# Decode attention, forward and backward: V transposes moved behind the K scores, fp32-pair transposes, and O and dq by wide matmuls

## The chip, the cores and the metric

The kernel runs on one core of one Trainium2 chip. The metric is the device time of one execution in microseconds. A profiled execution also has a span, from its first to its last instruction, which is a little shorter than its time.

## The reference

One query row meets 8192 keys in each of 32 heads, in bfloat16. The kernel returns the attention output O and the gradients of q, k and v.

```python
B, H, Sq, Skv, Dh = 1, 32, 1, 8192, 128
scores = jnp.einsum('bhqd,bhkd->bhqk', q, k) * q.shape[-1] ** -0.5
attn = softmax(scores)                        # p
out  = jnp.einsum('bhqk,bhkd->bhqd', attn, v) # O
out, vjp = jax.vjp(f, q, k, v); grads = vjp(grad_out)
```

Written out for one head, with dO for `grad_out`: dp = V dO, ds = p (dp - dO.O) x scale, dq is the sum of ds times the rows of K, dK is the outer product of ds and q, and dV the outer product of p and dO. A head reads K and V, 2.1 MB each, and writes dK and dV, 2.1 MB each; all else is small.

## The kernel before, in words

A head's K (or V) lies in SBUF as a tile of 128 partitions x 64 slots x 128 features: partition `p` holds the rows 64p to 64p+63. Softmax weights and scores of a head are 128 x 64. The loop (lines 228 to 296) runs over the heads, one more time than there are heads: iteration h works on head h up to dp, and finishes head h-1 (ds, dq, dK). The order of all instructions is the order of the source, since a manual schedule is entered at line 125; each engine takes its own instructions in that order.

In one iteration:

- VectorE transposes K in blocks of 32 x 32 words (`k_blocks`, line 133), and TensorE makes the K scores of it by 64 matmuls of four moving columns (`k_scores`, line 145). A mask on VectorE (`s_mask`, line 151) and eight short matmul passes (`s_swap`, line 161) put the scores in place.
- V has to be transposed on TensorE for dp, since V is contracted over features there. `v_transposes` (lines 165 to 172) does a quarter of the head: 16 transposes of 128 x 128 bfloat16 into a PSUM tile `T_ps` (two buffers), and one copy by ScalarE into `XT_sb` (three buffers). `v_scores` (line 180) then makes 16 columns of dp, by one matmul each, with dO as a moving operand of one column. Before the change the first two quarters of V's transposes stand ahead of the K scores, the other two after the softmax.
- The maximum over partitions goes by a diagonal matrix and an fp32 matmul with ones (`diag`, lines 251 to 254, and `nbias`, line 265). ScalarE makes the exponentials `e` and their row sums `rs` (line 268); an fp32 matmul with ones gives the whole sum (line 271), VectorE its reciprocal `rinv`, ScalarE the weights `p_rep`, each repeated R = 4 times (line 280).
- O of a head and dq of the head before come from `contract` (line 185): 64 matmuls each, V or K as the stationary operand of 128 x 128, one moving column. dq stands in two halves between the softmax steps; O stands between the third and fourth V transposes. A matmul with a broadcast dO (line 288) gives dO.O to all partitions.
- VectorE makes dK and dV in quarters (`outer`, line 195). After the second and the fourth quarter the SyncE queue stores half of the tensor (1.05 MB, line 203).

All DMAs are issued by SyncE, in source order. In the steady state its order in one iteration is: dK store, K load for head h+2 (line 258), dK store, dV store, V load for head h+2 (line 294), dV store. A load waits until its buffer is free: three buffers hold K, two hold V. A DMA further back on SyncE's queue waits behind it. K and V of the first two heads are asked for ahead of the loop, head 0 in four parts, and so is V of the last head.

Of the kernel before, what the change touches and what calls it, by code (L numbers as in the profile page):

```python
# [11 lines left out]
BF16 = mybir.dt.bfloat16  # L12
F32 = mybir.dt.float32
PSUM = bass.MemoryType.PSUM

CH = 16
R = 4
# [7 lines left out]
def kernel(  # L25
# [11 lines left out]
    nc = tc.nc  # L37
    P = 128
    _, H, S, D = k.shape
    assert D == P and S % (P * CH) == 0 and H <= P  # L40
    NT = S // P
# [3 lines left out]
    W = D // 2  # L45
# [3 lines left out]
    consts = ctx.enter_context(tc.tile_pool(name="consts", bufs=1))  # L49
# [3 lines left out]
    tpool = ctx.enter_context(tc.tile_pool(name="tsb", bufs=3))  # L53
    gpool = ctx.enter_context(tc.tile_pool(name="gen", bufs=2))
    small = ctx.enter_context(tc.tile_pool(name="small", bufs=2))
    psT = ctx.enter_context(tc.tile_pool(name="psT", bufs=2, space=PSUM))
# [4 lines left out]
    Kt, Vt, XK, XV, st = {}, {}, {}, {}, {}  # L61
# [9 lines left out]
    def load_k(h):  # L71
        Kt[h] = kpool.tile([P, NT, D], BF16, tag="K", name="Kt")
        parts = NCH if h == 0 else 1
        for c in range(parts):
            nc.sync.dma_start(slots(Kt[h], c, parts), rows_of(k, h, c, parts))  # L75

    def load_v(h):
        Vt[h] = vpool.tile([P, NT, D], BF16, tag="V", name="Vt")
        parts = NCH if h in (0, H - 1) else 1
        for c in range(parts):  # L80
            nc.sync.dma_start(slots(Vt[h], c, parts), rows_of(v, h, c, parts))

    rows = consts.tile([H, 2, D], BF16)
# [7 lines left out]
    ident = consts.tile([P, P], BF16)  # L91
    make_identity(nc, ident[:])
    ident_f = consts.tile([P, P], F32)
# [10 lines left out]
    for w in range(NB):  # L104
        for e2 in range(2):
            four = consts.tile([H, NQ, QD], BF16, tag=f"four{w}{e2}")
# [3 lines left out]
            tp = psT.tile([P, CH, P], BF16, tag="T")  # L110
# [1 line left out]
            nc.vector.tensor_tensor(  # L112
                q_blk[:, :, 2 * w + e2, :], tp[:, 0, 0:H].unsqueeze(2).to_broadcast([P, H, NQ]),
                in_quad[:].unsqueeze(1).to_broadcast([P, H, NQ]), op=ALU.mult)
    doT = consts.tile([P, H], BF16)
    do_f = consts.tile([P, H], F32)
    tp = psT.tile([P, CH, P], BF16, tag="T")
    nc.tensor.transpose(tp[:, 0, 0:H], rows[:, 1, :], ident[0:H, 0:H])
    nc.vector.tensor_copy(doT[:], tp[:, 0, 0:H])
    nc.vector.tensor_copy(do_f[:], doT[:])  # L120

    o_all = consts.tile([P, H], F32)
    dq_all = consts.tile([P, H], F32)
# [39 lines left out]
                             start=True, stop=True, skip_group_check=True)  # L163

    def v_transposes(h, c):
        T_ps = psT.tile([P, CH, P], BF16, tag="T", name="T_ps")
        for i in range(CH):
            nc.tensor.transpose(T_ps[:, i, :], Vt[h][:, c * CH + i, :], ident[:])  # L168
        X = tpool.tile([P, CH, P], BF16, tag="XT", name="XT_sb")
        nc.scalar.copy(X.rearrange("p c s -> p (c s)").bitcast(F32),  # L170
                       T_ps.rearrange("p c s -> p (c s)").bitcast(F32))
        XV[h, c] = X

    def v_scores(h, c):
        X = XV.pop((h, c))
        if c == 0:
            st[h]["dp"] = psD.tile([P, 512], F32, tag="dp", name="dp_ps")
        for i in range(CH):
            n = c * CH + i
            nc.tensor.matmul(st[h]["dp"][:, n:n + 1], lhsT=X[:, i, :], rhs=doT[:, h:h + 1],  # L180
                             start=True, stop=True, skip_group_check=True)

    def contract(Xt, rep, out_col, first=0, last=NT):
        for n in range(first, last):
            nc.tensor.matmul(out_col, lhsT=Xt[:, n, :], rhs=rep[:, n, 0:1],  # L185
                             start=(n == 0), stop=(n == NT - 1), skip_group_check=True)

    def outer(h, which, r):
        x = st[h]
        if r == 0:  # L190
            x[which] = gpool.tile([P, NT, D], BF16, tag=which, name="G_" + which)
        G, dst = x[which], out_2 if which == "dk" else out_3
        rep, row = x["ds"] if which == "dk" else x["p"], x["qd"][:, 0 if which == "dk" else 1, :]
        Q = NT // 4
        nc.vector.tensor_tensor(  # L195
            slots(G, r, 4).rearrange("p n (a b) -> p n a b", b=R),
            slots(rep, r, 4).unsqueeze(2).to_broadcast([P, Q, D // R, R]),
            row.rearrange("p (a b) -> p a b", b=R).unsqueeze(1).to_broadcast([P, Q, D // R, R]),
            op=ALU.mult)
        parts = 4 if h == H - 1 else NST  # L200
        if r % (4 // parts) == 4 // parts - 1:
            c = r // (4 // parts)
            nc.sync.dma_start(rows_of(dst, h, c, parts), slots(G, c, parts))

    def rows_bc(h):
        x = st[h]
        nc.tensor.matmul(x["m"][:, 256:512], lhsT=ident[0:H, h:h + 1].to_broadcast([H, P]),  # L207
                         rhs=rows[:].rearrange("h a d -> h (a d)"), start=True, stop=True,
                         skip_group_check=True)
        x["qd"] = small.tile([P, 2, D], BF16, tag="qd", name="qd")  # L210
        nc.scalar.copy(x["qd"][:].rearrange("p a d -> p (a d)"), x["m"][:, 256:512])
# [7 lines left out]
            out=x["ds"][:], in0=x["dp"][:, 0:NT].unsqueeze(2).to_broadcast([P, NT, R]), scalar=pdt[:],  # L219
            in1=x["p_s"][:].unsqueeze(2).to_broadcast([P, NT, R]), op0=ALU.subtract, op1=ALU.mult)  # L220

    def dq_of(h, half):
        out = st[h]["dp"][:, 128:129]
        contract(Kt[h], st[h]["ds"], out, half * NT // 2, (half + 1) * NT // 2)
        if half == 1:
            nc.scalar.copy(dq_all[:, h:h + 1], out)  # L226

    for h in range(H + 1):
        p_ = h - 1
        if h < H:  # L230
            x = st[h] = {}
            for u in range(NCH):
                k_blocks(h, u)
            v_transposes(h, 0)
            v_transposes(h, 1)
            k_scores(h)
            v_scores(h, 0)
        if h > 0:
            ds_of(p_)
            outer(p_, "dk", 0)  # L240
        if h < H:
            s_mask(h)
            s_swap(h)
        if h > 0:
            dq_of(p_, 0)
            outer(p_, "dk", 1)
        if h < H:
            mx = small.tile([P, 1], F32, tag="mx")
            nc.vector.reduce_max(mx[:], x["sn"], axis=AX.X)  # L249
            diag = small.tile([P, P], F32, tag="diag")  # L250
            nc.vector.tensor_scalar(diag[:], ident_f[:], mx[:], scale, op0=ALU.mult, op1=ALU.mult)  # L251
            x["m"] = psM.tile([P, 512], F32, tag="m", name="m_ps")
            nc.tensor.matmul(x["m"][:, 128:256], lhsT=ones_f[:], rhs=diag[:], start=True, stop=True,  # L253
                             skip_group_check=True)
        if h > 0:
            dq_of(p_, 1)
        if 0 < h and h + 2 < H:
            load_k(h + 2)
        if h > 0:
            outer(p_, "dk", 2)  # L260
        if h == 0:
            load_k(2)
        if h < H:
            nbias = small.tile([P, 1], F32, tag="nbias")
            nc.vector.tensor_reduce(nbias[:], x["m"][:, 128:256], axis=AX.X, op=ALU.max, negate=True)
            e = small.tile([P, NT], F32, tag="e")
            rs = small.tile([P, 1], F32, tag="rs")
            nc.scalar.activation(e[:], x["sn"], ACT.Exp, bias=nbias[:], scale=scale, accum_out=rs[:])
            rows_bc(h)
            v_scores(h, 1)  # L270
            nc.tensor.matmul(x["m"][:, 0:1], lhsT=ones_f[:], rhs=rs[:], start=True, stop=True,  # L271
                             skip_group_check=True)
        if h > 0:
            outer(p_, "dk", 3)
        if h == H:
            break
        rinv = small.tile([P, 1], F32, tag="rinv")
        nc.vector.reciprocal(rinv[:], x["m"][:, 0:1])  # L278
        x["p"] = small.tile([P, NT, R], BF16, tag="prep", name="p_rep")
        nc.scalar.activation(x["p"][:], e[:].unsqueeze(2).to_broadcast([P, NT, R]), ACT.Copy, scale=rinv[:])  # L280
        x["p_s"] = small.tile([P, NT], F32, tag="p_s", name="p_s")
        nc.vector.tensor_scalar(x["p_s"][:], e[:], rinv[:], scale, op0=ALU.mult, op1=ALU.mult)
        v_transposes(h, 2)
        contract(Vt[h], x["p"], x["m"][:, 2:3])
        nc.scalar.copy(o_all[:, h:h + 1], x["m"][:, 2:3])
        v_scores(h, 2)
        v_transposes(h, 3)
        nc.tensor.matmul(x["m"][:, 1:2], lhsT=do_f[:, h:h + 1].to_broadcast([P, P]), rhs=o_all[:, h:h + 1],
                         start=True, stop=True, skip_group_check=True)
        v_scores(h, 3)  # L290
        outer(h, "dv", 0)
        outer(h, "dv", 1)
        if h + 2 < H:
            load_v(h + 2)
        outer(h, "dv", 2)
        outer(h, "dv", 3)

# [2 lines left out]
    for src, dst in ((o_all, out_0), (dq_all, out_1)):  # L300
        half = small.tile([P, H], BF16, tag="half")
# [36 lines left out]
```

## Time and profile before

| | |
|---|---|
| median of 12 runs | 675.89 us (673.4 to 679.41) |
| the profiled execution: time | 676.35 us |
| its span | 674.6 us |
| mean granted TensorE clock | 0.574 |
| bytes read from and written to HBM | 134.23 MB and 134.23 MB, 398 GB/s over the span |
| busy: PE, weight loads (PEld), DVE, ACT | 522.3, 495.7, 508.7, 175.8 us |
| V transposes (line 168) | 2048, 232.2 us busy, 310 ns each from start to end |
| ScalarE's copies of them (line 170) | 128, 1012 ns each |
| dK and dV multiplies (line 195) | 256, about 1220 ns each |
| K block transposes (line 133) | 128, 1213 ns each |
| one-column matmuls for O and dq (line 185) | 2 x 2048, 165 ns each from start to end |

PE, DVE, ACT and SP are TensorE, VectorE, ScalarE and SyncE. A group's line in the profile gives the source line, the engine, the operation, the tile written and the tiles read. Since matmuls overlap, the time from start to end of one is longer than the distance between two; the busy time of PE is the union of them, and it is not a measure of how much of the array's throughput is used. The granted clock is the share of full speed that TensorE was given. A wait names the engine and line that waited, what ended the wait, the total in us, how many times, and the longest. The DMA share is the mean busy share of the core's 16 DMA engines. The chain is followed backwards from the last instruction, at each step to what released it.

### The profile page before, as it was taken

To read this page: it belongs to the slowest core of one execution; us is meant where nothing else is said; L and a number is where in the kernel's file an instruction comes from. 1 tells how busy PE (TensorE), PEld (TensorE's weight loads), DVE (VectorE), ACT (ScalarE), POOL (GpSimd) and SP (SyncE) were. 2 spreads that over 40 slices of the span, in tenths; PEclk is the share of its full clock that TensorE was granted. 3 is DMA by queue.
4 is the path that set the end of the run, shared out by engine and by line. 5 is a ranking of instruction groups with operands and counts; after the bars stand their busy time and mean duration, and the time that the engine had idled before them with its cause. 6 is when DMAs were issued, how large, how long until landed. Compare 5 with 4: busy or idle time off the path is not lost.

```text
span 674.6 us, 23039 instructions
## 1 busy us (share of the span) xinstructions
PE 522.3 (77%) x10727; PEld 495.7 (73%) x10727; DVE 508.7 (75%) x658; ACT 175.8 (26%) x321; POOL 0.7 (0%) x6
## 2 busy tenths in 40 slices
PE   3899898877779777779767787778877778666991
PEld 3888887867778777778667786767867678666881
DVE  4789888777787777877777866787677886669683
ACT  1333223222323222222222222223222222222330
POOL 0000000000000000000000000000000000000000
PEclk9555556666556665566655565556666555655565
DMA  8999999999999999999999999999999999999874
GB/s 335 420 417 421 425 426 422 427 425 425 425 427 423 426 426 424 426 424 418 423 409 394 387 413 393 397 389 397 416 405 408 410 394 409 395 392 380 341 319 179
DMA packets 29808, 269.96 MB, mean 400 GB/s; under 512 B 3472, under 2 KB 3472, under 8 KB 6032
## 3 DMA queue, kind: packets, MB, share of 16 engines
q1 hardware_dynamic: 29712, 268.48, 97.2%
q8 instruction: 84, 1.38, 0.8%
q14 instruction: 12, 0.10, 0.0%
HBM read 134.23 MB, written 134.23 MB: 398 GB/s over the span
## 4 chain that ended last, share of the span: by engine, by line
DMA 51%; PE 39%; DVE 6%; issue 1%; ACT 1%; SPq 0%
DMA Vt<-in_v_dram 51%; PE T_ps L168 20%; PE m_ps L185 5%; PE s_ps L145 5%; DVE G_dk L195 4%; PE dp_ps L180 3%; PE dp_ps L185 2%; PE m_ps L253 2%; PE m_ps L271 2%; DVE sm L151 1%; PE m_ps L207 1%; ACT XT_sb L170 1%; DVE diag L251 1%; DVE mx L249 0%; SPq L75 0%
## 5 line engine op out<-in xcount | busy, mean ns | idle before, releaser
L168 PE MATMUL T_ps<-ident,Vt 128*128 128x128 bf16 x2048 | 232.2, 310 | 86.3 <-DMA Vt<-in_v_dram 85.7
L168 PEld LDWEIGHTS <-Vt 128*128 128x128 bf16 x2048 | 215.3, 149 | 89.1 <-DMA Vt<-in_v_dram 88.3
L170 ACT COPY XT_sb<-T_ps 128x1024 f32<-128x1024 f32 x128 | 129.6, 1012 | 293.7 <-PE T_ps L168 293.7
L195 DVE TENSOR_TENSOR G_dk<-ds_rep,qd 128x2048 bf16<-128x2048 bf16 x128 | 155.7, 1219 | 1.1
L195 DVE TENSOR_TENSOR G_dv<-p_rep,qd 128x2048 bf16<-128x2048 bf16 x128 | 148.2, 1221 | 9.1 <-ACT p_rep L280 8.8
L133 DVE STREAM_TRANSPOSE XK_sb<-Kt 128x1024 f32<-128x1024 f32 x128 | 148.1, 1213 | 2.8 <-DMA Kt<-in_k_dram 2.8
L151 DVE TENSOR_TENSOR sm<-s_ps,in_quad 128x256 f32<-128x256 f32 x32 | 13.6, 425 | 107.4 <-PE s_ps L145 107.4
L180 PE MATMUL dp_ps<-doT,XT_sb 128*128 128x1 bf16 x2048 | 73.8, 165 | 26.8 <-ACT XT_sb L170 24.9
L180 PEld LDWEIGHTS <-XT_sb 128*128 128x128 bf16 x2048 | 64.1, 103 | 37.5 <-ACT XT_sb L170 27.6
L185 PEld LDWEIGHTS <-Kt 128*128 128x128 bf16 x2048 | 63.6, 102 | 6.9 <-issue 2.5
L185 PE MATMUL dp_ps<-ds_rep,Kt 128*128 128x1 bf16 x2048 | 64.6, 165 | 1.4 <-issue 0.9
L185 PEld LDWEIGHTS <-Vt 128*128 128x128 bf16 x2048 | 61.1, 105 | 0.0
L185 PE MATMUL m_ps<-p_rep,Vt 128*128 128x1 bf16 x2048 | 60.5, 166 | 0.0
L145 PE MATMUL s_ps<-q_blk,XK_sb 128*128 128x4 bf16 x2048 | 57.7, 167 | 0.0
L145 PEld LDWEIGHTS <-XK_sb 128*128 128x128 bf16 x2048 | 57.6, 100 | 0.0
L226 ACT COPY dq_all<-dp_ps 128x1 f32<-128x1 f32 x32 | 5.1, 159 | 136.1 <-PE dp_ps L185 136.1
L253 PE MATMUL m_ps<-diag,ones_f 128*128 128x128 f32 x64 | 24.3, 482 | 11.1 <-DVE diag L251 11.1
L253 PEld LDWEIGHTS m_ps<-diag,ones_f 128*128 128x128 f32 x64 | 15.2, 296 | 13.9 <-DVE diag L251 13.9
L280 ACT ACTIVATE p_rep<-e,rinv 128x256 bf16<-128x256 f32 x32 | 16.2, 508 | 29.9 <-DVE rinv L278 29.9
L278 DVE RECIPROCAL rinv<-m_ps 128x1 f32<-128x1 f32 x32 | 5.4, 169 | 24.1 <-PE m_ps L271 24.1
L218 DVE SCALAR_TENSOR_TENSOR ds_rep<-dp_ps,pdt,p_s 128x256 bf16<-128x256 f32 x32 | 15.5, 484 | 4.4 <-PE dp_ps L180 1.1
L271 PE MATMUL m_ps<-rs,ones_f 128*128 128x1 f32 x64 | 18.5, 358 | 0.3 <-issue 0.3
(40 smaller groups left out, 161.8 us busy)
## 6 DMA issues: line engine op xcount, KB each, us to landing
Kt<-in_k_dram SPq DMA_DIRECT2D x31, 2048.0 KB, 22.1
out_dram<-G_dv SPq DMA_DIRECT2D x62, 1024.0 KB, 23.5
out_dram<-G_dk SPq DMA_DIRECT2D x62, 1024.0 KB, 20.0
Vt<-in_v_dram SPq DMA_DIRECT2D x30, 2048.0 KB, 25.3
Vt<-in_v_dram SPq DMA_DIRECT2D x8, 512.0 KB, 13.8
Kt<-in_k_dram SPq DMA_DIRECT2D x4, 512.0 KB, 5.3
out_dram<-G_dv SPq DMA_DIRECT2D x4, 512.0 KB, 11.6
out_dram<-G_dk SPq DMA_DIRECT2D x4, 512.0 KB, 9.6
```

Source lines behind the costliest of these rows:

```text
L133: nc.vector.transpose(XK[h][:, :, :, u, :], slots(Kt[h], u, NCH).rearrange("p g d -> p (g d)").bitcast(F32).rearrange("p (g w j) -> p g w ...
L145: nc.tensor.matmul(out[:, g, :], lhsT=cols[:, g, c // 2, c % 2], rhs=q_blk[:, h, c, :], start=(c == 0), stop=(c == 2 * NB - 1), skip_group ...
L151: nc.vector.tensor_tensor(x["sm"][:], x["s"][:, 0:NT].rearrange("p (a g) -> p a g", a=NQ).unsqueeze(2) .to_broadcast([P, NQ, NCH, CH]), in ...
L168: nc.tensor.transpose(T_ps[:, i, :], Vt[h][:, c * CH + i, :], ident[:])
L170: nc.scalar.copy(X.rearrange("p c s -> p (c s)").bitcast(F32), T_ps.rearrange("p c s -> p (c s)").bitcast(F32))
L180: nc.tensor.matmul(st[h]["dp"][:, n:n + 1], lhsT=X[:, i, :], rhs=doT[:, h:h + 1], start=True, stop=True, skip_group_check=True)
L185: nc.tensor.matmul(out_col, lhsT=Xt[:, n, :], rhs=rep[:, n, 0:1], start=(n == 0), stop=(n == NT - 1), skip_group_check=True)
L195: nc.vector.tensor_tensor(slots(G, r, 4).rearrange("p n (a b) -> p n a b", b=R), slots(rep, r, 4).unsqueeze(2).to_broadcast([P, Q, D // R, ...
L218: nc.vector.scalar_tensor_tensor(out=x["ds"][:], in0=x["dp"][:, 0:NT].unsqueeze(2).to_broadcast([P, NT, R]), scalar=pdt[:], in1=x["p_s"][: ...
L253: nc.tensor.matmul(x["m"][:, 128:256], lhsT=ones_f[:], rhs=diag[:], start=True, stop=True, skip_group_check=True)
L271: nc.tensor.matmul(x["m"][:, 0:1], lhsT=ones_f[:], rhs=rs[:], start=True, stop=True, skip_group_check=True)
L280: nc.scalar.activation(x["p"][:], e[:].unsqueeze(2).to_broadcast([P, NT, R]), ACT.Copy, scale=rinv[:])
```

## The change

The K scores come first in an iteration, and all V transposes come after the softmax weights. dq is dealt out in four unequal parts (4, 5, 4 and 3 of 16 matmuls) between the softmax steps. V is transposed as 32-bit words that hold two neighbouring features: 32 transposes of 128 x 128 words take the place of 64, and `v_scores` reads the even and the odd halves of the words, with `do_blk`, a zero-padded dO, so that two matmuls add up to two columns of dp. The number of those matmuls (64) stays.

O and dq go by `contract_wide`: four columns of weights (one for each of four slots) are stationary, and four slots of V or K (512 columns) move, 16 matmuls a head, into four rows of a whole PSUM bank: the bank of the head's scores for O, that of dp for dq. The four diagonal blocks of 128 are wanted; `gather_wide` copies the four rows to SBUF by ScalarE and adds the blocks by four fp32 matmuls. The last head keeps the old `contract`. V of head h+1 is loaded at the start of iteration h, behind both dV stores of head h-1, in place of V of head h+2 between the dV stores of head h. The K load stands after the fourth part of dq.

```diff
     def v_transposes(h, c):
-        T_ps = psT.tile([P, CH, P], BF16, tag="T", name="T_ps")
-        for i in range(CH):
-            nc.tensor.transpose(T_ps[:, i, :], Vt[h][:, c * CH + i, :], ident[:])
-        X = tpool.tile([P, CH, P], BF16, tag="XT", name="XT_sb")
-        nc.scalar.copy(X.rearrange("p c s -> p (c s)").bitcast(F32),
-                       T_ps.rearrange("p c s -> p (c s)").bitcast(F32))
+        T_ps = psT.tile([P, CH // 2, P], F32, tag="T", name="T_ps")
+        words = Vt[h].rearrange("p n d -> p (n d)").bitcast(F32)
+        for i in range(CH // 2):
+            m = c * CH // 2 + i
+            nc.tensor.transpose(T_ps[:, i, :], words[:, m * P:(m + 1) * P], ident_f[:])
+        X = tpool.tile([P, CH // 2, P], F32, tag="XT", name="XT_sb")
+        nc.scalar.copy(X[:], T_ps[:])
...
+    def contract_wide(Xt, rep, bank, first, last):
+        for g in range(first, last):
+            nc.tensor.matmul(bank[0:R, :], lhsT=rep[:, R * g:R * (g + 1), 0],
+                             rhs=Xt[:, R * g:R * (g + 1), :].rearrange("p n d -> p (n d)"),
+                             start=(g == 0), stop=(g == NT // R - 1), skip_group_check=True)
+
+    def gather_wide(bank, out_col):
+        four = small.tile([R, R, D], F32, tag="four", name="four")
+        nc.scalar.copy(four[:].rearrange("a b d -> a (b d)"), bank[0:R, :])
+        for b in range(R):
+            nc.tensor.matmul(out_col, lhsT=four[:, b, :], rhs=ident_f[0:R, b:b + 1],
+                             start=(b == 0), stop=(b == R - 1), skip_group_check=True)
...
+    def dq_of(h, part):
+        dp, cuts = st[h]["dp"], (0, 4, 9, 13, 16)
+        if h < H - 1:
+            contract_wide(Kt[h], st[h]["ds"], dp, cuts[part], cuts[part + 1])
+            if part == 3:
+                gather_wide(dp, dp[:, 128:129])
+        else:
+            contract(Kt[h], st[h]["ds"], dp[:, 128:129], 4 * cuts[part], 4 * cuts[part + 1])
+        if part == 3:
+            nc.scalar.copy(dq_all[:, h:h + 1], dp[:, 128:129])
...
-            v_transposes(h, 0)
-            v_transposes(h, 1)
             k_scores(h)
-            v_scores(h, 0)
+            if 0 < h < H - 1:
+                load_v(h + 1)
...
+        broad = h < H - 1
+        v_transposes(h, 0)
+        if broad:
+            contract_wide(Vt[h], x["p"], x["s"], 0, 4)
+        else:
+            contract(Vt[h], x["p"], x["m"][:, 2:3])
+        v_transposes(h, 1)
+        if broad:
+            contract_wide(Vt[h], x["p"], x["s"], 4, 8)
+        v_scores(h, 0)
         v_transposes(h, 2)
-        contract(Vt[h], x["p"], x["m"][:, 2:3])
+        if broad:
+            contract_wide(Vt[h], x["p"], x["s"], 8, 12)
+        v_scores(h, 1)
+        v_transposes(h, 3)
+        if broad:
+            contract_wide(Vt[h], x["p"], x["s"], 12, 16)
+            gather_wide(x["s"], x["m"][:, 2:3])
         nc.scalar.copy(o_all[:, h:h + 1], x["m"][:, 2:3])
         v_scores(h, 2)
-        v_transposes(h, 3)
```

On TensorE an iteration is then: K scores, dq part 0, the swap of scores, dq part 1, the maximum's matmul, the rows of q and dO (`rows_bc`), dq part 2, the sum's matmul, dq part 3, the gather of dq, and then V transposes and O by quarters with dp between them, the gather of O, dO.O, and the rest of dp.

More of the change, by code (lines that the diff above doesn't have):

```diff
@@ L114 @@
                 in_quad[:].unsqueeze(1).to_broadcast([P, H, NQ]), op=ALU.mult)
-    doT = consts.tile([P, H], BF16)
+    do_blk = consts.tile([P, H, 2, 2], BF16)
+    nc.vector.memset(do_blk[:], 0.0)
+    for e2 in range(2):
+        twice = consts.tile([H, 2, W], BF16, tag=f"twice{e2}")
+        nc.vector.tensor_copy(
+            twice[:], rows[:, 1, :].rearrange("h (j e) -> h e j", e=2)[:, e2:e2 + 1, :].to_broadcast([H, 2, W]))
+        tp = psT.tile([P, CH, P], BF16, tag="T")
+        nc.tensor.transpose(tp[:, 0, 0:H], twice[:].rearrange("h t j -> h (t j)"), ident[0:H, 0:H])
+        for t in range(2):
+            nc.vector.tensor_copy(do_blk[t * W:(t + 1) * W, :, e2, t], tp[t * W:(t + 1) * W, 0, 0:H])
     do_f = consts.tile([P, H], F32)
@@ L118 @@
     nc.tensor.transpose(tp[:, 0, 0:H], rows[:, 1, :], ident[0:H, 0:H])
-    nc.vector.tensor_copy(doT[:], tp[:, 0, 0:H])
-    nc.vector.tensor_copy(do_f[:], doT[:])
+    nc.vector.tensor_copy(do_f[:], tp[:, 0, 0:H])
     o_all = consts.tile([P, H], F32)
@@ L165, in v_transposes @@
     def v_transposes(h, c):
-        T_ps = psT.tile([P, CH, P], BF16, tag="T", name="T_ps")
-        for i in range(CH):
-            nc.tensor.transpose(T_ps[:, i, :], Vt[h][:, c * CH + i, :], ident[:])
-        X = tpool.tile([P, CH, P], BF16, tag="XT", name="XT_sb")
-        nc.scalar.copy(X.rearrange("p c s -> p (c s)").bitcast(F32),
-                       T_ps.rearrange("p c s -> p (c s)").bitcast(F32))
+        T_ps = psT.tile([P, CH // 2, P], F32, tag="T", name="T_ps")
[5 more added lines that the diff above has]
+        nc.scalar.copy(X[:], T_ps[:])
         XV[h, c] = X
     def v_scores(h, c):
-        X = XV.pop((h, c))
+        X = XV.pop((h, c)).rearrange("p m s -> p (m s)").bitcast(BF16).rearrange("p (m s e) -> p m e s", s=P, e=2)
         if c == 0:
             st[h]["dp"] = psD.tile([P, 512], F32, tag="dp", name="dp_ps")
[L178 to L181, printed above, removed]
+        for i in range(CH // 2):
+            n = c * CH + 2 * i
+            for e2 in range(2):
+                nc.tensor.matmul(st[h]["dp"][:, n:n + 2], lhsT=X[:, i, e2, :], rhs=do_blk[:, h, e2, :],
+                                 start=(e2 == 0), stop=(e2 == 1), skip_group_check=True)
     def contract(Xt, rep, out_col, first=0, last=NT):
@@ L220, in ds_of @@
             in1=x["p_s"][:].unsqueeze(2).to_broadcast([P, NT, R]), op0=ALU.subtract, op1=ALU.mult)
[L222 to L226, printed above, removed]
+    def dq_of(h, part):
[8 more added lines that the diff above has]
+            nc.scalar.copy(dq_all[:, h:h + 1], dp[:, 128:129])
     for h in range(H + 1):
@@ L240 @@
             outer(p_, "dk", 0)
+            dq_of(p_, 0)
         if h < H:
@@ L244 @@
         if h > 0:
-            dq_of(p_, 0)
+            dq_of(p_, 1)
             outer(p_, "dk", 1)
@@ L254 @@
                              skip_group_check=True)
+            rows_bc(h)
         if h > 0:
[L256 to L259, printed above, removed]
+            dq_of(p_, 2)
             outer(p_, "dk", 2)
@@ L268 @@
             nc.scalar.activation(e[:], x["sn"], ACT.Exp, bias=nbias[:], scale=scale, accum_out=rs[:])
-            rows_bc(h)
-            v_scores(h, 1)
             nc.tensor.matmul(x["m"][:, 0:1], lhsT=ones_f[:], rhs=rs[:], start=True, stop=True,
@@ L273 @@
         if h > 0:
+            dq_of(p_, 3)
+            if h + 2 < H:
+                load_k(h + 2)
             outer(p_, "dk", 3)
@@ L292 @@
         outer(h, "dv", 1)
-        if h + 2 < H:
-            load_v(h + 2)
         outer(h, "dv", 2)
```

## The prediction

> **What bounds the kernel now.** I read the page first: the slices, the DMA queues and the chain.
>
> ```profile
> DMA  8999999999999999999999999999999999999874
> q1 hardware_dynamic: 29712, 268.48, 97.2%
> DMA 51%; PE 39%; DVE 6%; issue 1%; ACT 1%; SPq 0%
> ```
>
> The 16 DMA engines are full from the second slice to the 37th, and the chain runs through loads of V more than through any engine. Next I cut the span at starts of V transposes that had waited for V (every fourth head), and asked for engines, clock and DMA in each stretch.
>
> ```profile
> 201.63:283.92 82.29, 65.05 (x1340) 61.80 (x1341) 63.32 (x81) 21.79 (x40) 0.00 (x0) 0.58 1.01 425
> 367.61:453.29 85.68, 66.12 (x1340) 62.72 (x1341) 63.20 (x81) 21.77 (x40) 0.00 (x0) 0.52 1.00 396
> ```
>
> Columns: length, busy PE, weight loads, DVE, ACT, POOL, then clock, DMA share, GB/s. Four heads take 82.3 us (20.6 each) at 425 GB/s and 85.7 (21.4) at 396; the DMA share is 1.0 in both, so the head's 8.39 MB set the period. DVE has 15.8 us of work in a head. How far behind TensorE is, the waits tell:
>
> ```profile
> PE T_ps L168 <- DMA Vt<-in_v_dram: 85.7, 27, 4.5
> DVE sm L151 <- PE s_ps L145: 107.4, 32, 5.1
> ```
>
> 27 heads begin with about 3.2 us of waiting for V. In the first heads, not yet waiting, the chain has V transposes start at 27.20, 44.77 and 62.18: TensorE's own head is 17.4 us. So TensorE has 3 to 4 us to spare in a head, DVE 5, and the DMA none. The last V transposes that wait for their load start at 623.47; from there to the end (674.6) it is 51.1 us of engine work and a last store.
>
> [...]here six such windows of one head, of which I show four:
>
> ```profile
> 242.62:246.04 3.42, 3.27 (x31) 3.28 (x32) 1.85 (x4) 1.01 (x1) 0.00 (x0) 0.50 1.00 426
> 246.04:249.45 3.41, 3.29 (x123) 3.11 (x121) 1.56 (x3) 1.01 (x1) 0.00 (x0) 1.00 1.04 440
> 249.45:252.86 3.41, 3.03 (x59) 2.58 (x57) 2.88 (x5) 0.73 (x4) 0.00 (x0) 0.50 0.99 416
> 252.86:256.27 3.41, 3.41 (x82) 3.41 (x83) 2.93 (x5) 1.52 (x2) 0.00 (x0) 0.50 1.03 435
> ```
>
> 31 transposes (128 moving columns each) in a window bring clock 1.00 in the next; 123 matmuls of 1 to 4 columns bring 0.50 after it, though PE is "busy" in both. [...]A window from 454.25 with 25 transposes was followed by 1.00, one from 556.65 with 21 was not. [...]16 transposes in 1.73 us are 108 ns each.[...]
>
> **The change, part by part, in one head of TensorE.** Removed: 64 V transposes, 64 x 108 ns = 6.9 us; 2 x 64 one-column matmuls for O and dq, 2 x 1.68 us (chain rows of L185 x64) = 3.4 us. Together 10.3 us of the 17.4.
>
> Added: (a) 32 fp32 transposes. Rows for fp32 (L253, L271) show two passes for a matmul and some 214 ns from one pass to the next, whether 1 or 128 columns move[...]. Lower end 107 ns at half clock (one pass, load hidden), next 213 (load bound), upper 427 (two passes); I take 160, at full clock 80: 5.1 or 2.6 us. (b) 2 x 16 wide matmuls: 32 x 427 = 13.7 us at half clock, 32 x 216 = 6.9 at full. (c) Two gathers: each stops TensorE for ScalarE's copy of 4 x 512 words (between the 1012 ns of 1024 and the 159 ns of 1: 0.6 us, and 0.3 + 0.2 for the signals), then 4 fp32 matmuls of two passes: 8 x 214 = 1.7 us, estimate 0.9 at full clock. So 2.0 to 2.8 us each. All V transposes and O of the head are queued behind the first, the do.O matmul behind the second. On ScalarE p_rep is queued behind the dq copy, hence VectorE's dV multiplies too; VectorE's 5 us cover that. (d) dp stays 64 matmuls of 25 ns, now two columns wide: nothing.
>
> Sums, the two stages of a head as they stand in the new order. K stage at full clock: scores 1.65, mask and swap 0.9, maximum and diagonal 0.8, its matmul 0.6, bias, exp and sum 1.9, dq's last part 0.65, gather 2.0, some 0.5 of signals: 9.0 us; dq's other 13 matmuls (2.8 us) lie under VectorE's answers. V stage at full clock: transposes 2.6, O 3.5, dp 1.7, gather 2.0, do.O 0.5, wait for p_rep 0.3: 10.6. Sum 19.6 us; with transposes at 107 ns even at full clock, 20.4. At half clock only: K stage 13, V stage 16.5, 29.5 us.
>
> The clock decides. Wide matmuls and transposes fill the windows of the V stage, so the full clock comes there, but a window late: up to 3.4 us at half clock, 1.7 us lost. Whether the K stage (16 x 216 = 3.5 us of moving columns in 9.0) keeps it no row says[...]. I take the loss of one window in two heads of three: 19.6 + 1.15 = 20.75 us.
>
> **What moves besides.** V's load for head h+1 is asked for at the start of head h, behind both dV stores of h-1 instead of between them; on SP's queue it passes one store of 1.05 MB, 2.6 us later. But it is needed only in the V stage, some 32 us after its buffer is free instead of 20: the 85.7 us of waiting for V go. What is late next is TensorE itself. K's load still stands between the dK stores; it waits for dq's last part, 7 to 9 us into a head, as now (251.61 against 242.76). ScalarE's copies of transposes keep size and number; two copies of 0.6 us a head fit in its 74% idle time. The extra do_blk set-up (some 7 short VectorE copies of 0.17 to 0.2 us) costs 1.2 us at most, once, and lies partly beside K's first load. Bytes are the same.
>
> **Sum.** Start of scores 13 us (now transposes at 10.84, scores 14.0); head 0 without dq 20.75 - 2 = 18.75; 30 heads x 20.75 = 622.5; last head, O by the old narrow way, 19; last dq and dK 6 and last store 10, as now (658.9 to 674.6). Span 689.3. The profiled execution has a span of 674.6 and a time of 676.35, 1.75 outside; so 691 us. Its time lies 0.46 above the median of the 12 runs (675.89), which I neglect.
>
> **Rivals.**
> - A, the forecast: TensorE is the bound, at 20 to 21.5 us a head. For it: added work (at best 2.6 + 6.9 + 4.0 against 10.3 removed) uses up the 3 us that V's wait shows to be free. Own range 676 to 712. Chance 0.42.
> - B, the other side: the DMA stays the bound and the end shortens. From V's last awaited landing it is V stage 10.6, K stage 9, V stage 9, 6 and 10 = 44.6 us instead of 51.1; less 2.6 for the store that V now follows: 674.6 - 3.9 + 1.75 = 672 us. It decides if TensorE's head stays below the DMA's 19.7 to 21.4 us: full clock throughout, and transposes under 80 ns. Against it: the first half, at 425 GB/s, leaves nothing above 19.7. At the start V(2) is asked for 5 us later, under 5 us of stores; bare, that would cost up to 5 and end it level. The fall from 425 to 396 GB/s with the DMA share unchanged might also give way to another order of transfers, or grow; I count nothing. Range 664 to 678, chance 0.33.
> - C: the K stage falls back to half clock in every head, its streams then taking 11 to 12 us, and the V stage starts cold: 12. At 23.5 us a head 13 + 21.5 + 705 + 21 + 16 = 776.5, so 778; heads between A and C give 715 to 780. Chance 0.22.
> - D: fp32 transposes in two passes, 427 ns, mostly at half clock: 28 us a head and more, over 870 us. Chance 0.03.
>
> **Chances.** Under 0.3% a measurement of this kernel can't tell a change from none. B gives 0.21 of faster, 0.10 of same, 0.02 slower; A 0.01, 0.04 and 0.37; C and D are slower. Faster 0.22, same 0.14, slower 0.64. The range runs from B's low end, 664, to 750, which leaves out D and half of C.
>
> **What the profile would show.** Forecast right: DMA share clearly below 1.0 in mid-span, no wait for V, TensorE's heads at 20 to 21.5 us, the clock about 0.8. Of the steps: spacing of fp32 transposes near 160 or 80 ns; 512-column matmuls at 216 to 427; a ScalarE copy "four" of 0.6 us with TensorE idle before the gather. B: DMA share 1.0, TensorE waiting for something in each head. C: clock near 0.6 and heads of 23 us. I am wrong if the full clock holds through the K stage and transposes cost 54 ns, or if the gathers are far cheaper than 2 us.

## The result, and the profile after

The change makes the kernel slower: 728.66 us median of 8 runs against 676.14 us of the runs of the kernel before beside it, ratio 1.078 (95% interval 1.0755 to 1.0802). Forecast was 691, in a range of 664 to 750.

The profiled execution after has a span of 727.5 us. From its page, the engines, the granted clock, the DMA and the chain:

```profile
PE 657.1 (90%) x7225; PEld 403.5 (55%) x7225; DVE 514.0 (71%) x664; ACT 211.7 (29%) x383; POOL 0.7 (0%) x6
...
PEclk9998989978998998988899899897799989899787
DMA  8999999999999999999899999999989999999836
...
PE 81%; ACT 12%; DVE 3%; issue 1%; DMA 1%; SPq 0%; ACTq 0%
```

The chain has gone from DMA 51% and PE 39% to PE 81%. TensorE is the bound, at a clock of 0.875 instead of 0.574. The DMA line alone would mislead: its digits are still nines. The two hundred microseconds in mid-span (same columns as in the prediction: length, PE, PEld, DVE, ACT, POOL, clock, DMA share, GB/s) say more, first before, then after.

```profile
325.00:525.00 200.00, 156.12 (x3202) 147.95 (x3202) 147.35 (x189) 51.24 (x94) 0.00 (x0) 0.55 1.01 402
```

```profile
325.00:525.00 200.00, 186.35 (x2005) 113.66 (x2004) 141.84 (x178) 59.46 (x108) 0.00 (x0) 0.87 0.97 379
```

The DMA share falls only from 1.01 to 0.97 though the engines move 6% less; but a K load now lands 10.2 us after it is issued where it took 22.1, and nobody waits for V any more. The waits of after (engine and line, what it waited for, us in all, times, longest):

```profile
DVE G_dv L221 <- ACT p_rep L310: 68.0, 29, 2.7
PE m_ps L211 <- ACT four L209: 20.7, 31, 0.7
PE dp_ps L211 <- ACT four L209: 20.6, 31, 0.7
```

Most of what is left of TensorE's idle time in mid-span is the stop ahead of each gather, 0.67 us twice a head. The first K scores start at 13.46 us. From start to start, heads 1 to 30 take 21.2 to 24.0 us, 22.2 in the mean, of which 10.5 pass from the K scores to the first V transpose (the K stage) and 11.7 from there to the next K scores (the V stage). One of the slowest heads, from its chain:

```profile
319.76 1.67 PE s_ps L154 x64
321.44 1.06 PE dp_ps L203 x3
322.50 0.12 PE s_ps L170 x5
322.62 0.62 PE dp_ps L203
323.24 0.21 PE s_ps L170 x2
323.45 2.13 PE dp_ps L203 x5
325.58 0.73 PE m_ps L284 x2
...
329.02 0.58 ACT four L209
329.60 0.04 issue
329.64 1.12 PE dp_ps L211 x8
330.77 1.90 PE T_ps L180 x8
```

Columns: start, length on the chain, what. dq's first nine wide matmuls (L203) stand on the chain themselves, some 427 ns each: 1.06 + 0.62 + 2.13 us. So do the other seven, 1.19 and 0.75 us. In the traces of both kernels the granted clock is 0.5 or 1.0, and each recorded stretch at one of them, but for the last, lasts a whole multiple of 3.413 us; such a piece of 3.413 us is called a window here. The clock was at a half for two windows, from 320.25 to 327.07 us (the clock is the third number from the end):

```profile
316.84:320.24 3.40, 2.73 (x68) 2.62 (x68) 1.79 (x4) 0.87 (x3) 0.00 (x0) 1.00 1.02 424
320.25:323.66 3.41, 3.41 (x58) 2.03 (x55) 2.87 (x5) 0.00 (x0) 0.00 (x0) 0.50 1.04 440
323.67:327.06 3.39, 3.39 (x10) 1.19 (x9) 1.51 (x3) 0.37 (x1) 0.00 (x0) 0.50 0.98 411
```

Then comes the stop for the copy "four", the gather, and V transposes that again begin at half clock, 1.90 us for eight where full clock takes 1.02. This last loss is found in four of the 30 heads only, those of 24.0 us. In the other 26 the V stage has the full clock throughout and takes 11.46 us. The K stage has one window at half clock in 15 heads (9.7 to 10.2 us) and two in the other 15 (about 11.0 us).

### The profile page after: what moved, and what is told of

It reads as the page before. It is cut to its first block, busy times and chain, and to the rows that moved or that the text cites. A ratio compares the mean times of both kernels' runs of the same rounds, so it can differ in the third digit from the quotient of the medians.

```text
span 727.5 us, 16204 instructions
## 1 busy us (share of the span) xinstructions
PE 657.1 (90%) x7225; PEld 403.5 (55%) x7225; DVE 514.0 (71%) x664; ACT 211.7 (29%) x383; POOL 0.7 (0%) x6
## 4 chain that ended last, share of the span: by engine, by line
PE 81%; ACT 12%; DVE 3%; issue 1%; DMA 1%; SPq 0%; ACTq 0%
PE dp_ps L203 19%; PE T_ps L180 17%; PE s_ps L203 13%; PE dp_ps L192 8%; PE s_ps L154 7%; ACT four L209 5%; PE dp_ps L211 5%; PE m_ps L211 4%; ACT XT_sb L182 4%; PE m_ps L284 3%; PE m_ps L298 2%; ACT e L297 2%; PE s_ps L170 1%; ACT qd L237 1%; PE m_ps L233 1%
## 5 line engine op out<-in xcount | busy, mean ns | idle before, releaser
L203 PE MATMUL dp_ps<-Kt,ds_rep 128*4 128x512 bf16 x496 | 182.0, 507 | 0.0
L180 PE MATMUL T_ps<-ident_f,Vt 128*128 128x128 f32 x1024 | 142.9, 284 | 0.0
L203 PE MATMUL s_ps<-Vt,p_rep 128*4 128x512 bf16 x496 | 130.6, 387 | 0.0
L180 PEld LDWEIGHTS T_ps<-ident_f,Vt 128*128 128x128 f32 x1024 | 113.5, 144 | 15.2 <-issue 14.8
L203 PEld LDWEIGHTS <-ds_rep 128*4 128x4 bf16 x496 | 43.0, 103 | 64.2 <-issue 49.7
L192 PE MATMUL dp_ps<-do_blk,XT_sb 128*128 128x2 bf16 x2048 | 70.3, 164 | 0.0
L203 PEld LDWEIGHTS <-p_rep 128*4 128x4 bf16 x496 | 32.5, 85 | 55.6 <-issue 24.3
L211 PE MATMUL dp_ps<-ident_f,four 4*128 4x1 f32 x248 | 32.8, 249 | 20.6 <-ACT four L209 20.6
L211 PE MATMUL m_ps<-ident_f,four 4*128 4x1 f32 x248 | 32.5, 248 | 20.7 <-ACT four L209 20.7
L211 PEld LDWEIGHTS dp_ps<-ident_f,four 4*128 4x128 f32 x248 | 30.1, 187 | 36.3 <-ACT four L209 36.3
L294 DVE TENSOR_REDUCE nbias<-m_ps 128x1 f32<-128x128 f32 x32 | 9.3, 292 | 46.2 <-ACT qd L237 46.2
## 6 DMA issues: line engine op xcount, KB each, us to landing
Kt<-in_k_dram SPq DMA_DIRECT2D x31, 2048.0 KB, 10.2
out_dram<-G_dv SPq DMA_DIRECT2D x62, 1024.0 KB, 10.6
```

Source lines behind the costliest of these rows:

```text
L180: nc.tensor.transpose(T_ps[:, i, :], words[:, m * P:(m + 1) * P], ident_f[:])
L192: nc.tensor.matmul(st[h]["dp"][:, n:n + 2], lhsT=X[:, i, e2, :], rhs=do_blk[:, h, e2, :], start=(e2 == 0), stop=(e2 == 1), skip_group_chec ...
L203: nc.tensor.matmul(bank[0:R, :], lhsT=rep[:, R * g:R * (g + 1), 0], rhs=Xt[:, R * g:R * (g + 1), :].rearrange("p n d -> p (n d)"), start=( ...
L211: nc.tensor.matmul(out_col, lhsT=four[:, b, :], rhs=ident_f[0:R, b:b + 1], start=(b == 0), stop=(b == R - 1), skip_group_check=True)
```

## The experiments

Two theories stood at the start. W: the wide matmuls and their gathers make TensorE the bound. O, the rival: the new order, or V's later load, costs the time by itself. A third, T, blames the fp32 transposes.

### Taking the wide matmuls back

In e1 both `broad` and the condition in `dq_of` are set so that all heads use `contract`; e3 does it for dq alone, e4 for O alone.

```diff
-        if h < H - 1:          # in dq_of
+        if h < 0:
-        broad = h < H - 1
+        broad = False
```

> New order, new V load place and fp32-pair transposes kept; O and dq of all heads by the old 64 one-column matmuls, no gathers. Theory W (wide matmuls and gathers are what costs): TensorE's head falls from 22.1 us by some 32 x 0.27 + 2 x 1.7 - 3.4 = 8.6 us, to 14 to 16.5 us, far under the DMA's 19.7 to 21.4; the DMA is full again and the time is 665 to 680 us, V's waits gone. Rival O (the new order itself, or V's later load, costs): the time stays above 700 us.

Measured 662.17 us, ratio to the kernel before 0.9773 (0.9731 to 0.9814). O is refuted: without the wide matmuls the same order is faster than the kernel before.

> The change with dq alone by the old narrow matmuls, O wide with its gather. Theory W: the head loses dq's 16 wide matmuls (4.6 us, over half of them at half clock), its gather (1.7) and gains 1.7: 22.1 - 4.6 = 17.5 us, under the DMA's period: 670 to 685 us. Rival O: above 700.

> The change with O alone by the old narrow matmuls, dq wide with its gather. O's wide matmuls ran at full clock: 3.5 us, the gather 1.7, against 1.7 narrow: 22.1 - 3.5 = 18.6 us if the clock stays; without O's moving columns the transposes may fall to half clock (3.5 us more), giving up to 22. So 670 to 725 us, and a lower clock than 0.875.

Measured 676.81 us (0.9975, 0.9962 to 0.9988) and 679.11 us (1.0011, 0.9992 to 1.0029), within both expectations. One wide contraction a head costs 15 to 17 us over none, two cost 66: with one, TensorE's head (20.48 us in both) just reaches the DMA's period (20.4 us in e1 from head 12 on), and what the second adds can no longer hide. The clock fell to 0.756 and 0.762.

### Taking the fp32 pairs back

In e2 `v_transposes` and `v_scores` are those of the kernel before; in e8 too, with O and dq narrow, so that the order alone is left.

> The change with V transposed as bfloat16 as before (64 a head, dp by one-column matmuls); all else as changed. If fp32 pairs save TensorE time: 64 x 56 to 64 ns against 32 x 109 ns at full clock are level (3.6 to 4.1 against 3.5 us a head), so 725 to 745 us by theory W. If fp32 transposes are the fault (rival T): below 710 us.

Measured 723.24 us, ratio 1.0663 (1.0607 to 1.0719), a little under what was expected. T is refuted: from start to start at full clock, bfloat16 transposes are 56 ns apart in the trace of before and the fp32 ones of the change 109 ns, so 64 of the one and 32 of the other are the same work.

> The new order and load place alone: bfloat16 transposes, narrow O and dq. TensorE's head about 17 us against 14 to 16.5 with fp32 pairs at half clock (64 x 107 against 32 x 213 ns: level), both under the DMA's period. So as the first experiment, 658 to 667 us: the fp32 pairs do nothing. If the pairs are what made that kernel fast: 670 us or more.

Measured 667.09 us (0.9822, 0.9801 to 0.9842), at the edge of the expectation. The order carries the gain over the kernel before. The pairs give another 5 us here (662 against 667), and cost as much beside the wide matmuls (729 against 723); no run shows by what.

### The stops at the gathers

In e5 the copy stays, the four fp32 matmuls move:

```diff
+            st[h]["four"] = gather_copy(dp)      # where gather_wide stood
...
         v_transposes(h, 0)
+        dq_end(p_)                               # the matmuls, and the copy to dq_all
...
+            four = gather_copy(x["s"])
+        v_scores(h, 2)
+        gather_add(four, x["m"][:, 2:3])
```

> The change, with ScalarE's two copies of four rows issued where they were and their fp32 matmuls moved behind the next TensorE work: those of dq behind the first V transposes, those of O behind a quarter of dp; do.O last. If TensorE's idle time before the gathers (20.6 + 20.7 us in the trace of the change) and the short waits at the head's end are on the path: 40 to 55 us less, 675 to 690 us. If something else of the same length stands behind them: above 715 us.

Measured 677.3 us (0.9985, 0.9973 to 0.9997): 51 us less than the change, all that was expected and more than the 41 us of idle time. The rest goes with a clock of 0.916: in e5 a head has one window at half clock, in the change 1.6 in the mean. p_rep comes earlier, too; what that is worth was not taken apart. In e5 nearly every head takes 20.48 us.

### The clock

> The change with 29 extra matmuls of 256 columns a head, whose results nobody reads, in the stretch that moves few columns (from O's gather to the end of the K scores). They take 29 x 107 = 3.1 us at full clock, 0.4 of it in idle time. Clock theory: the full clock holds through dq's first parts (216 ns for 512 columns instead of 427), saves 1.9 us a head: mean clock over 0.95 and a time of 728 + 31 x (2.7 - 1.9) = 740 to 755 us. Rival (the clock there is not set by moved columns): 728 + 31 x 2.7 = 812 us or more, clock as before.

Measured 938.15 us (1.3805), clock 0.824: neither theory's number. One filler matmul was put behind every four narrow ones of the K scores. TensorE's timeline of e6 (start, length, engine, line, ...) shows what that did:

```profile
411.62 0.26 PE L159 MATMUL s_ps<-q_blk,XK_sb 128*128 128x4 bf16 x4
411.81 0.27 PE L148 MATMUL s_ps<-Kt,ident 128*4 128x256 bf16 x1
412.01 0.26 PE L159 MATMUL s_ps<-q_blk,XK_sb 128*128 128x4 bf16 x4
```

From 411.62 to 412.01 is 0.39 us for 4 x 25 + 110 = 210 ns of matmuls (blocks of 8 and of 6 fillers take 1.04 and 0.82 us in e11's trace, so one more is 110 ns): changing from one kind to the other and back costs 0.18 us here. The filler slowed everything down, and the clock still fell, from the change's 0.875 to 0.824. So the run doesn't decide between the theories. e11 repeats it with the filler in blocks:

```diff
+                fill(h, x["s"][0:R, 192:448], 6)      # in k_scores, at g = 5 and 10
...
+            fill(h, x["m"][0:R, 256:512], 4)          # ahead of O's gather
             gather_wide(x["s"], x["m"][:, 2:3])
+            fill(h, x["m"][0:R, 256:512], 8)
...
         v_scores(h, 2)
+            fill(h, x["m"][0:R, 256:512], 6)
...
         v_scores(h, 3)
+            fill(h, x["m"][0:R, 256:512], 8)
```

> The change with filler columns once more, now in blocks: 4 matmuls of 256 columns before O's gather, 8 behind it, 6 and 8 after the last quarters of dp, 6 and 6 inside the K scores; nobody reads their results. Some 3.6 us of columns a head at full clock and about 1.2 us for changing kind. Clock theory: [...]the full clock holds to dq's end: mean clock over 0.95, dq's 512-column matmuls 216 ns apart throughout, 728 + 31 x (4.8 - 1.9) = 820 us. Rival: clock as in the change (0.875), dq's first parts at 427 ns, 875 us or more.

Measured 821.54 us (1.2107, 1.2066 to 1.2148), clock 0.968. The first dq matmuls of a head, in the timelines of the change and of e11:

```profile
321.37 1.44 PE L203 MATMUL dp_ps<-Kt,ds_rep 128*4 128x512 bf16 x3
323.24 2.34 PE L203 MATMUL dp_ps<-Kt,ds_rep 128*4 128x512 bf16 x5
```

```profile
415.34 0.81 PE L210 MATMUL dp_ps<-Kt,ds_rep 128*4 128x512 bf16 x3
416.32 1.24 PE L210 MATMUL dp_ps<-Kt,ds_rep 128*4 128x512 bf16 x5
```

The same three and five matmuls take 0.81 and 1.24 us once blocks of filler columns move ahead of them, 26 x 256 a head from O's gather to the end of dp and 12 x 256 in the K scores. So with these columns in the stretch of O's gather, dp, do.O and K scores, the matmuls behind it had the full clock that they lack in the change. Not every form of filler does that, as e6's 0.824 shows.

### What else could have stood on the path

> The change with the rows of q and dO (one matmul and ScalarE's copy of 0.37 us) back behind the exponentials. In the change VectorE's nbias waits for that copy (46.2 us in all). If this lies on TensorE's path: 0.4 to 0.6 us a head less, 710 to 718 us. If dq's part 2 covers it (TensorE is busy then): within 4 us of the change.

Measured 734.4 us, ratio 1.0824 (1.0787 to 1.086): 6 us more than the change, outside both expectations. In the profiled execution heads 1 and 3 take 26.1 us; from head 4 on a head takes 22.2 us in the mean, as in the change. So the place of the rows brings nothing, and why two early heads are slower is not shown. VectorE's wait for ScalarE's copy is long (46.2 us), but little of it reaches TensorE: in the change it waits 7.0 us in all for the exponentials that follow, since dq's part 2 keeps it busy meanwhile.

In e12 the V stage is `v_transposes` 0 and 1, eight wide matmuls, dp 0 and 1, and the same once more.

> The change with its V stage in larger blocks: two quarters of V transposes, O's 8 wide matmuls, two quarters of dp, and the same again; the same instructions, four changes of kind fewer. In the trace a block of 8 transposes takes 1.02 us for 8 x 109 ns and a block of 4 wide matmuls 0.96 for 4 x 216, so a change of kind costs some 0.12 us: 4 x 0.12 x 31 = 15 us less, 710 to 718 us. If changes of kind cost nothing, or the transposes wait for ScalarE's copies instead: 725 us or more.

Measured 709.72 us (1.0436, 1.0392 to 1.0479), 19 us less than the change. The V stage at full clock goes from 11.46 to 10.98 us. By the source the edit saves five changes of kind in it, from nine to four, and not four as was expected: 0.1 us each, 15 us in all. The rest goes with a clock of 0.887 instead of 0.875. In e12's timeline 16 transposes take 1.89 us, from 299.90 to 301.79:

```profile
299.90 1.97 PE L180 MATMUL T_ps<-ident_f,Vt 128*128 128x128 f32 x16
301.79 1.89 PE L203 MATMUL s_ps<-Vt,p_rep 128*4 128x512 bf16 x8
303.61 0.95 PE L192 MATMUL dp_ps<-do_blk,XT_sb 128*128 128x2 bf16 x32
```

e14 joins e5 and e12:

> The change with both repairs: the gathers' fp32 matmuls behind other work and the V stage in larger blocks. Alone they gave 51 and 19 us. If they add, TensorE's head falls to about 19.8 us, level with the DMA's at 425 GB/s: 655 to 668 us, as fast as narrow matmuls in the same order. If TensorE's half-clock windows and wide columns still bind: 670 us or more.

Measured 656.51 us (0.9744, 0.971 to 0.9777), clock 0.928, and 426 GB/s from 325 to 525 us. The two repairs add up, 51 + 19 of 72 us. They bring the rate up to that of the fastest runs here, but the chain of e14 is still TensorE's:

```profile
PE 80%; DVE 8%; ACT 7%; DMA 3%; issue 1%; SPq 0%; DVEq 0%
```

So wide matmuls can be had for nothing, but they bring nothing over the narrow ones of e1 and e9.

### Why the order is worth something

Between 325 and 525 us e1 moves 422 GB/s where the kernel before moves 402. e9 is e1 with V's load for head h+2 back between the dV stores; e10 is the kernel before with that load behind both of them.

> The first experiment (new order, fp32 pairs, narrow O and dq: 662.17 us), with V of head h+2 again asked for between the dV stores of head h. It tells why that kernel kept 425 GB/s to 525 us where the kernel before fell to some 400 from 325 us on. If the place of V's load among the stores holds the rate: the rate falls again and the time is 670 us or more. If the order of compute (K scores first, V needed later) does: within 4 us of 662.

> The kernel before with one edit: V of head h+2 is asked for behind both dV stores of head h instead of between them. If the place of the load among the stores holds the DMA rate: 660 to 668 us, 425 GB/s past 325 us. If not: V, needed at once in this order, comes 2.6 us later and the time is 676 to 690 us.

Measured 659.12 us (0.971, 0.9684 to 0.9736) and 680.9 us (1.0022, 0.9991 to 1.0054). The place of the load among the stores is not it: with the old place e9 keeps 425 GB/s, with the new one e10 has 397. e13 gives the kernel before a longer lead only (a third buffer, and V asked for one head earlier):

```diff
-V_BUFS = 2
+V_BUFS = 3
...
-        if h + 2 < H:
-            load_v(h + 2)
+        if h + 3 < H:
+            load_v(h + 3)
```

> The kernel before with a third buffer for V and V asked for one head earlier (head h+3 at the end of head h); nothing else. The new order with narrow matmuls gives V's load half a head more before it is needed and holds 422 to 425 GB/s between 325 and 525 us, where the kernel before has 402. If the longer lead alone does it: no wait for V, the rate at 420 or more, 655 to 668 us. If the order of TensorE's work matters in itself: the rate stays near 400 and the time above 670 us.

Measured 661.31 us (0.9812, 0.9786 to 0.9837). The stretch from 325 to 525 us in e9, in e10 and in e13:

```profile
325.00:525.00 200.00, 159.42 (x2998) 147.16 (x2996) 157.44 (x196) 53.35 (x96) 0.00 (x0) 0.59 1.01 425
```

```profile
325.00:525.00 200.00, 151.34 (x3070) 143.79 (x3068) 146.66 (x186) 50.21 (x92) 0.00 (x0) 0.54 1.00 397
```

```profile
325.00:525.00 200.00, 163.93 (x3270) 153.35 (x3266) 155.20 (x196) 54.45 (x100) 0.00 (x0) 0.53 1.01 424
```

A longer lead between V's request and its use brings the rate up: e13 shows it for a third buffer. That the new order works in the same way, by using V later in the head, is concluded from this and was not taken apart. In the trace of the kernel before it is the loads that slow down: their packets of 16 KB take 0.68 us in the mean from 325 to 525 us and 0.62 from 100 to 300 us, while the stores' packets of 8 KB keep 0.31. Why a short lead does this to a DMA that is busy all the time is not shown.

## Why the prediction was right in kind and wrong in size

The mechanism of case A came true: V's wait went, and TensorE became the bound. Its size did not. For 20 to 21.5 us a head 22.2 came, and 728.66 lies above A's own range (676 to 712), in the stretch between A and C. A part of C is there, too: the K stage falls to half clock in every head, though not for all of its length, and the mean clock is 0.875 where A said about 0.8 and C near 0.6. That the stated range held the result is due to its reaching halfway into C. 14.6 us more than the profiled execution were forecast (691 against 676.35), some 52 came. By the sum's own lines:

| term | forecast | measured |
|---|---|---|
| start of the K scores | 13 | 13.5 |
| head 0 | 18.75 | 19.4 |
| 30 heads | 30 x 20.75 = 622.5 | 30 x 22.19 = 665.7 |
| last head and end | 19 + 16 = 35 | 28.9 |
| span | 689.3 | 727.5 |

So all of the error, and 5 us more, lies in the 20.75 us of a head, 19.6 plus 1.15 for the clock. At full clock the K stage's 9.0 us were right: heads of e14 that lose no window have a K stage of 7.07 us without the gather, 8.8 with the gather's 1.7. Two terms failed. The V stage at full clock was put at 10.6 us and takes 11.46. And half clock, put at 1.15 us a head, takes what is left of 22.2, some 1.9.

- "I take 160, at full clock 80" for an fp32 transpose: wrong. From start to start in the trace they are 213 ns apart at half clock and 109 at full. The upper neighbour, "213 (load bound)", had the right number, though no run shows that the load sets it: 32 x 29 ns = 0.9 us a head, some 28 us in all. For the wide matmuls the forecast's 427 and 216 ns are what the trace of after shows at half and at full clock; the trace of before had no matmul of 512 columns.
- "dq's other 13 matmuls (2.8 us) lie under VectorE's answers": the step of the K stage that failed. It holds at full clock only. At half clock nine of them take 3.8 us. In the head from 319.76 VectorE has the diagonal ready at about 324.1 us, TensorE ends dq's part 1 only at 325.5, and the maximum's matmul waits behind it. The cover was worked out at full clock, for a stage that runs half of its time without it.
- "I take the loss of one window in two heads of three": too few. Heads 1 to 30 have 49 windows at half clock, 1.6 a head instead of 0.67. Of the wide matmuls that follow each other at one clock, about a quarter (180 of 690 pairs) do so at half clock; of 992 that is some 255 x 0.21 us = 54 us, 1.7 a head.
- Missing altogether: a price for changing between kinds of matmul. e12 puts it at 0.1 us; among transposes, O and dp the V stage has nine such changes, some 0.9 us.
- The gathers, put at 2.0 us each at full clock, take 1.7 to 1.8 (1.05 to 1.12 us of matmuls, 0.67 of stop with the signals). That p_rep, and VectorE's dV, wait behind them was said; that they also stand in the stretch that loses the clock was not.
- The last head and the end were put 6 us too long, which by luck hides a part of the error.

Rival B named one point that the sum then counted at nothing: the fall of the rate from 425 to 396 GB/s can be undone, as e1 shows with 662 us. But it does not "give way to another order of transfers" (e9 and e10 speak against that); a longer lead for V's load does it in e13. The change hides this gain, as TensorE doesn't ask for 425 GB/s. Counted from e1, the wide matmuls and gathers cost 66 us; moving the gathers takes 51 off the change (e5), larger blocks 19 (e12), both together 72 (e14).

## What to carry to other kernels

Before a faster-looking shape takes the place of many short matmuls, price it at the slow clock too (here 427 ns for a wide matmul, 216 at the full one), and then ask at which clock the stretch ahead of it leaves TensorE; here one of narrow matmuls and waits left it at half in each of heads 1 to 30. Work that is to hide under another engine's answer has to be costed at the clock of that place: dq's nine matmuls took 3.8 us at half, where 9 x 216 ns = 1.9 had been counted on. Needing a transfer later in the loop can be worth more than work saved on an engine (e13, with a third V buffer and V asked for one head earlier, takes 661.31 us against 674.41): look at the rate in each stretch (402 and 424 GB/s here), not at the busy share of the DMA (1.01 beside both).

## What the runs showed of the hardware that had not been expected

- How many columns moved in a window, and what the clock was in the next, was counted from the starts of the matmuls in the traces of both kernels between 27 and 630 us; a column of an fp32 transpose is counted twice, since 128 of them take 213 ns at half clock where 128 of bfloat16 take 107. In the kernel before, the 23 windows at half clock that were followed by the full one moved 3,059 columns or more; the 130 others at most 2,687, but for one with 3,073. In the change, the 102 windows that kept the full clock moved 3,138 or more, the 30 that lost it at most 2,938. On the way up the change doesn't separate: 30 windows with 3,183 or more were followed by the full clock, and 13 with up to 3,239 were not. What the clock goes by, beyond these counts, is not shown.
- With gathers later (e5) nearly every head takes 20.48 us, six windows of 3.413 us, and the change repeats a pattern of eight heads every 177.5 us, 52 windows. That the heads lock to the windows is an inference from these numbers; no run tried it.
- Narrow matmuls (the K scores, four columns) hardly feel the clock: in the change 27 ns from start to start at half, 25 at full.
- A DMA share of 1.0 stood beside 397, 402 and 424 GB/s (e10, the kernel before and e13).
